# The second products of the last but one group in Strassen's form: a change at the end of a fused block kernel

## The chip, the cores and the metric

The kernel runs on one core of a Trainium2 chip. The metric is the device time of one execution in microseconds (us); smaller is better. Each time below is either that device time or a time in the trace of one profiled execution, counted from the start of its span.

The engines that matter here are TensorE (PE in the profile; its weight loads are PEld), VectorE (DVE), ScalarE (ACT), GpSimd (POOL) and SyncE (SP). PE writes its products into banks of its accumulator memory. There are eight, and each holds a tile of 128 x 512 numbers. DVE and ACT read them from there into the large on-chip memory. DMAs move data between that memory and DRAM, and one kind, issued from POOL, adds what it carries to what lies at its destination.

## The reference

The block is an FNet layer followed by a gated feed-forward layer, both with adaptive layer norms, for 2048 rows of 512 features and 1792 hidden features:

```python
x = A_x
mod = (_silu(c) @ w_mod).reshape(c.shape[0], 6, 1, -1)
sa, ca, ga, sb, cb, gb = (mod[:, 0], mod[:, 1], ..., mod[:, 5])
h = _layernorm(x) * (1 + ca) + sa
x = x + ga * _A_ref(h, ...)          # two DFTs as matrix products
h = _layernorm(x) * (1 + cb) + sb
gate = h @ w1
up = h @ w3
x = x + gb * ((_silu(gate) * up) @ w2)
```

The change lies wholly in the last line: `(silu(h @ w1) * (h @ w3)) @ w2`, scaled by `gb` and added to `x`.

## The kernel before

**Tiles.** Everything is held with features on the 128 partitions and rows along the free dimension. The 2048 rows are four tiles `t` of 512 rows. They go in two pairs, `PAIRS = ((0, 2), (1, 3))`. The 1792 hidden features are seven groups `g` of 256 (`NG` is 7), and the 512 output features are four columns `d` of 128 (`ND` is 4). Every product is made from three matmuls (`PASSES`): each operand is split into a high part, rounded by a copy on ACT, and a low part, the difference, taken on DVE.

**First products and second products.** An item `(g, pair)` is one group of hidden features for one pair of row tiles. Its first products are `h @ w1` and `h @ w3` for two row tiles and two blocks of 128 hidden features: eight block products in the plain form, seven in Strassen's form (in Winograd's order), with sums of operands formed ahead and sums of results formed behind. Most items make both in the seven-product form. These are the units `a1` to `a7` (w1) and `b1` to `b7` (w3) in the code, each of six matmuls. `result` takes what they give: it applies Silu to the gate, multiplies the two, and splits the product into high and low, as the operand of the second product.

**The second products** multiply that by `w2`. There are two forms:
- `down_unit`, the plain form: eight units for an item, one for each row tile `t` and output column `d`, each of six matmuls into one bank. Which bank is chosen by a counter, `turn[1]`, that only this function advances, modulo the length of the list `down_banks`. That list is `[6, 7]` during most of the phase and `[6, 7, 0, 1, 2]` from the last `a` unit of the last item on. The counter has advanced eight times for each item in this form.
- `seven_unit`, Strassen's form: seven units, in the order `ORDER7 = (2, 5, 3, 1, 6, 7, 4)`, each of six matmuls, three into bank 6 and then three into bank 7. Units 2, 5 and 1 begin a new sum in the two banks, and the units after each of them add to it. After every unit ACT copies both banks, scaled by `gb`, into a tile `y`, and POOL issues a DMA that adds `y` to its destination. `seven_parts` forms the seven right operands from the four results of the item, and `seven_jobs` prepares w2 for it: five jobs, against two in the plain form (`plain_jobs`).

`SEVEN` lists the items whose second products have Strassen's form: pair 1 and groups 0 to 4. The last two items, `(5, 1)` and `(6, 1)`, go by `down_unit`, in a form of their own (`own`): the running sum of `x` for row tiles 1 and 3, which till then lies in DRAM (`sums`), has been loaded into four tiles `xr` by `load_sums`, and DVE adds each bank to `xr` with one instruction. In the last item each such sum is followed at once by the DMA that writes it to the output.

**The order of the work** is written out by hand. For each item the strings `head` and `body` in the loop at the end of `folded` list the units: `a6` is unit 6 of w1 of this item, `-b7` is unit 7 of w3 of the item before, and `y` is the next unit of the queue `seconds`. That queue is filled after an item's unit `b3`: with seven entries for an item in `SEVEN`, otherwise with eight. Every engine then runs its instructions in the order in which the code issued them, and waits at the first that isn't ready.

Within a unit the order is this: `delayed()` first issues what earlier units put off (`behind(k, f)` has `f` run at the start of the k-th unit after this), then the six matmuls, then the reading of the bank, and last `beside`, which issues a few preparing jobs from the queue `jobs` if their estimated costs fit a budget of the unit. So the split of the `b3` results into high parts, put off by one unit, stands on ACT ahead of the copies of the next unit.

The preparation of w3 for the next item (`weight_jobs(i + 1, "w3")`: a high part, four short sums, a low part, the high and the low part of the sums) is put in the queue after `b6`.

`judge` compares sums of squares, collected earlier, that decide whether the fast form of the kernel was allowed; it is a chain of short DVE instructions and one memset on POOL. It runs at the unit at which nine second products of the last item's queue are left.

Of the kernel before, what the change touches and what calls it, by code (L numbers as in the profile page):

```python
# [12 lines left out]
OP = mybir.AluOpType  # L13
# [8 lines left out]
NT = S // N  # L22
ND = D // P
NG = F // (2 * P)
# [18 lines left out]
def folded(nc, pools, c, cp, wmr, wmc, x, xt, ctr, cti, wdr, wdi, w1, w3, w2, out):  # L43
# [39 lines left out]
    def cols(i):  # L83
        return slice(i * P, (i + 1) * P)
# [27 lines left out]
    done = set()  # L112
# [683 lines left out]
    xr = {}  # L796
# [17 lines left out]
    PAIRS = ((0, 2), (1, 3))  # L814
    h2h, h2l = {}, {}
    xc, sums = {}, {}
# [308 lines left out]
    def down_unit(g, pair, t, d, key):  # L1125
        last = g == NG - 1

        own = pair == 1 and g >= NG - 2
        if not own and d % 2 == 0:
            ys[0] = take(F32, "y")  # L1130

        parts = 2 if own and last and (t, d) == (NT - 1, ND - 1) else 1
        for n in range(parts):
            at = slice(n * N // parts, (n + 1) * N // parts)
            to = bank(down_banks[turn[1] % len(down_banks)])[:, at]
            turn[1] += 1
            for q in range(2):
                product(
                    to,
                    [u[:, q, cols(d)] for u in wuse[key]],  # L1140
                    [hf[g, t, q][:, b, at] for b in range(2)],
                    q == 0,
                    q == 1,
                )
            if own:
                xs = xr[t][d // 2][:, d % 2, at]
                nc.vector.scalar_tensor_tensor(
                    xs, to, gb[:, d : d + 1], xs, op0=OP.mult, op1=OP.add
                )
                if last:  # L1150
                    nc.sync.dma_start(out[t, d, :, at], xs)
            else:
                if pair == 0 and 1 <= g * ND + d <= 4:
                    nc.vector.tensor_scalar(
                        ys[0][:, d % 2, :], to, gb[:, d : d + 1], None, op0=OP.mult
                    )
                else:
                    copy_by(ys[0][:, d % 2, :], to, gb[:, d : d + 1])
        if not own and d % 2 == 1:
            y = ys.pop(0)  # L1160
            nc.gpsimd.dma_start(sums[t, d // 2], y, accum_op=OP.add)  # L1161
            behind(4, lambda: give(y))
            if last:
                behind(8, lambda i=d // 2: store(t, i))
        if d == ND - 1:
            for q in range(2):
                give(hf.pop((g, t, q)))
            if t == PAIRS[pair][1]:
                give_w(key)
            if pair == 1 and g == NG - 3:  # L1170
                load_sums(t)
# [51 lines left out]
    TO = {1: 0, 6: 0, 7: 0, 4: 0, 2: 1, 5: 2, 3: 2}  # L1223
    state, vs = {}, {}

    SEVEN = [(g, 1) for g in range(NG - 2)]
    ORDER7 = (2, 5, 3, 1, 6, 7, 4)
    LEFT7 = {1: "h0", 2: "h2", 4: "h3", 5: "s0", 6: "s1", 7: "s2", 3: "s3"}
    TO7 = {2: (0, 0), 5: (1, 1), 3: (0, 1), 1: (0, 0), 6: (0, 1), 7: (1, 1), 4: (1, 0)}
# [101 lines left out]
    def seven_unit(g, pair, n, key):  # L1331
        new = n in (1, 2, 5)
        if new:
            banks7[:] = [bank(6), bank(7)]
        y = take(F32, "y")
        which, k = TO7[n]
        t = PAIRS[pair][k]
        names = ("h", "l") if LEFT7[n][0] == "h" else ("sh", "sl")
        u = right7.pop(((g, pair), n))
        for e, to in enumerate(banks7):  # L1340
            at = int(LEFT7[n][1]) * HALF + e * P
            product(
                to,
                [flat(wuse[key][x])[:, at : at + P] for x in names],
                [u[:, b, :] for b in range(2)],
                new,
                True,
                not new,
            )
            d = 2 * which + e  # L1350
            copy_by(y[:, e, :], to, gb[:, d : d + 1])
        give(u)
        nc.gpsimd.dma_start(sums[t, which], y, accum_op=OP.add)  # L1353
        behind(4, lambda: give(y))
        if n == ORDER7[-1]:
            for x in wuse.pop(key).values():
                give(x)
            if g == NG - 3:
                for t in PAIRS[pair]:
                    load_sums(t)  # L1360
# [330 lines left out]
    def beside(us, used):  # L1691
        advance(us - used[0], us - used[1], jobs)
        if not jobs:
            advance(0.0, 0.0)
# [9 lines left out]
    def down(g, pair, *which):  # L1704
        key = which[-1]
        drain(lambda: (key, "l") in done, jobs)
        delayed()
        if (g, pair) in SEVEN:
            seven_unit(g, pair, *which)
        else:  # L1710
            down_unit(g, pair, *which)
        beside(1.36, USED["own" if pair == 1 and g >= NG - 2 else "y"])

    for w in ("w1", "w3"):
        load_w((w, 1))
# [33 lines left out]
    def early_w3(i):  # L1749
        return items[i][1] == 1  # L1750

    def unit(kind, i, n):
        g, pair = items[i]
        more = i + 1 < len(items)
        if n == 1:
            drain(lambda: ("ready", i, "w1" if kind == "a" else "w3") in done, jobs)
        if (kind, i, n) == ("a", 0, 6):
            drain(lambda: ("t", 0, 4) in done)
        if (kind, i, n) == ("a", turning, 1):
            drain(lambda: not background)  # L1760
        if kind == "a" and i == turning and n in (4, 5, 6, 7):
            drain(lambda: ("t", 1, {6: 2, 5: 1, 7: 3, 4: 4}[n]) in done, jobs)
        delayed()
        factor(i, "w1" if kind == "a" else "w3", n)
        if (kind, n) == ("a", 1):
            load_w(("w1", *items[i + 1]) if more else ("w2", g, pair))
        if (kind, n) == ("a", 6):
            load_w(("w2", g, pair))
        if not more and kind == "a" and state[i, "w1"]["n"] == 7:
            down_banks[:] = [6, 7, 0, 1, 2]  # L1770
        if (kind, n) == ("a", 7 if i == turning else 3) and more:
            load_w(("w3", *items[i + 1]))
            weight_jobs(i + 1, "w1")
        if (kind, n) == ("b", 2):
            (seven_jobs if (g, pair) in SEVEN else plain_jobs)(("w2", g, pair))
        if (kind, n) == ("b", 3):
            if i + 2 == turning:
                drain(lambda: ("xc", 3) in done)
                for at in ((1, 0), (1, 1), (3, 1)):
                    chunk_parts(background, *at, 3)  # L1780
                sums_of.append(pair_sums(background, 1))
            if i + 1 == turning:
                other_operands()
            if more and not early_w3(i):
                weight_jobs(i + 1, "w3")
            if (g, pair) in SEVEN:
                seconds.extend((g, pair, n, ("w2", g, pair)) for n in ORDER7)
            else:
                for t in PAIRS[pair]:
                    seconds.extend((g, pair, t, d, ("w2", g, pair)) for d in range(ND))  # L1790
        if (kind, n) == ("b", 6) and more and early_w3(i):
            weight_jobs(i + 1, "w3")
        beside(1.36, FACTOR[kind][n])

# [3 lines left out]
    for i in range(len(items)):  # L1798
        body = "a6 a5 y y a7 y a3 y a4 y b1 y b2 y b6 b5 y"
        if i and items[i - 1] in SEVEN:  # L1800
            body = "a6 a5 a7 y a3 a4 y b1 b2 y b6 b5 y"
        if i == turning + 1:
            body = "a6 a5 y a7 a3 y a4 b1 y b2 b6 y b5"
        spread = i > 1 and items[i - 2] in SEVEN
        if spread and i < len(items) - 1:
            body = body.replace("a6", "a6 y", 1)
        if i == len(items) - 2:
            body = "a6 y a5 y a7 a3 y a4 b1 y b2 b6 y b5"
        if i == turning:
            body = "y y y y y a6 y a5 y a7 y b1 b2 a4 b6 a3 b5"  # L1810
        if i == len(items) - 1:
            body = "a6 a5 b1 a7 a3 b2 a4 y b6 y b5 y b7 y b4 y y b3 y y y y y y y y y y"
        head = "-b7 a1 -b4 -b3 a2 " if i == turning else "-b7 a1 a2 -b4 -b3 " if i else "a1 a2 "
        if spread and i < len(items) - 1:
            head = "-b7 a1 y a2 -b4 y -b3 "
        if i == len(items) - 1:
            head = "-b7 y a1 a2 y -b4 y -b3 "
        for at in (head + body).split():
            if at == "y":
                if (i, len(seconds)) == (len(items) - 1, 9):  # L1820
                    judge()
                if (i, len(seconds)) == (len(items) - 1, 4):
                    tc.mark_branch_hint_location("general", hint="LikelyTaken")
                down(*seconds.popleft())
            elif at[0] == "-":
                unit(at[1], i - 1, int(at[2]))
            else:
                unit(at[0], i, int(at[1]))
# [804 lines left out]
```

## Time and profile before

| what | value |
|---|---|
| device time, median of 3 runs | 691.38 us |
| lowest and highest of the 3 | 690.79 and 692.02 us |
| device time of the profiled execution | 690.63 us |
| span of its trace | 688.8 us |
| PE busy | 672.4 us, 98% of the span |
| DVE busy | 586.8 us, 85% |
| ACT busy | 451.2 us, 65% |
| POOL busy | 132.2 us, 19% |
| mean rate of the DMAs | 170 GB/s |

The device time holds about 1.8 us more than the span, which runs from the first to the last event of the trace. PE is busy nearly all the time. Its busy time is only a rough measure, because matmuls overlap: a matmul of 512 columns is shown with some 390 ns, but the next one starts some 227 ns after it. How well PE is used is therefore read from the starts of the matmuls, in the view that lists instructions in order of time.

A line of that view gives the start in us, the duration in us, the engine, the line of the code, the operation, the tile written and the tiles read, the shapes, the count, and in brackets the idle time of the engine before it with what ended it.

### The profile page before, as it was taken

Reading aid. Unit: us, or ns where it says so; the run is one execution under the profiler, and the core shown is the slowest. Engines: PE = TensorE matmul, PEld = TensorE weight load, DVE = VectorE, ACT = ScalarE, POOL = GpSimd, SP = SyncE. Lnnn points to the kernel's source line nnn. Section 1 sums busy time; section 2 is a strip of 40 time slices with the busy share of each in tenths; the row PEclk is TensorE's granted clock in tenths of the full one; section 3 lists DMA queues with packets and bytes.
Section 4 is the critical chain, followed back from the end, with each engine's and each line's share of the span. In section 5 each row is a group of like instructions: output and inputs, shape, how many; then the busy total and the mean of one; then the engine's idle time right before and its main releaser. Section 6 shows DMA issues by size and latency. Waiting matters only on the chain.

```text
span 688.8 us, 9035 instructions
## 1 busy us (share of the span) xinstructions
PE 672.4 (98%) x3122; PEld 557.4 (81%) x3122; DVE 586.8 (85%) x945; ACT 451.2 (65%) x751; POOL 132.2 (19%) x156
## 2 busy tenths in 40 slices
PE   6999999999999999999999999999999999999996
PEld 4898788888888888888788888887887888888785
DVE  5999769998999987989997989787998979888465
ACT  4998956455343665663577767867687887877620
POOL 1320162543435000100101001011011112221100
PEclk9999999999999999999999999999999999999998
DMA  8740299787679440274767666475859998999713
GB/s 264 224 124 1 54 368 339 249 297 258 197 287 291 154 151 30 46 139 122 119 141 141 150 153 121 94 128 118 267 108 183 175 203 167 181 214 173 179 45 127
DMA packets 40837, 116.80 MB, mean 170 GB/s; under 512 B 5200, under 2 KB 5456, under 8 KB 40784
## 3 DMA queue, kind: packets, MB, share of 16 engines
q0 software_dynamic: 14512, 50.86, 36.9%
q1 hardware_dynamic: 25840, 63.98, 28.1%
q10 hardware_dynamic: 432, 1.31, 0.6%
q8 instruction: 26, 0.43, 0.3%
q14 instruction: 27, 0.22, 0.1%
HBM read 76.81 MB, written 41.42 MB: 172 GB/s over the span
## 4 chain that ended last, share of the span: by engine, by line
PE 84%; DVE 9%; ACT 4%; issue 1%; DMA 1%; SPq 0%; DVEq 0%; ACTq 0%
PE bank L100 54%; PE bank L750 26%; PE bank L559 2%; PE bank L598 1%; ACT hm L501 1%; DMA x<-in_x 1%; DVE xr L806 1%; DVE st L449 1%; PE bank L576 1%; DVE v L96 1%; DVE hl L90 0%; DVE ul L90 0%; DVE x L93 0%; ACT hh L87 0%; DVE w3s L90 0%
## 5 line engine op out<-in xcount | busy, mean ns | idle before, releaser
L100 PE MATMUL bank<-hf,w2h 128*128 128x512 f32 (+1 forms) x352 | 108.3, 389 | 0.0
L87 ACT ACTIVATE hf<-v 128x512 fp32r<-128x512 f32 x71 | 44.4, 631 | 66.7 <-DVE v L96 53.9
L335 ACT ACTIVATE y<-bank,gb 128x512 f32<-128x512 f32 x118 | 76.5, 682 | 3.9 <-PE bank L100 3.6
L100 PEld LDWEIGHTS bank<-hf,w2h 128*128 128x128 f32 x352 | 65.6, 188 | 15.4 <-ACT y L335 1.5
L1161 POOL DMA_DIRECT2D sum<-y x28 | 24.0, 857 | 240.7 <-ACT y L335 124.5
L100 PE MATMUL bank<-hf,w2l 128*128 128x512 f32 (+1 forms) x176 | 68.1, 387 | 0.0
L90 DVE TENSOR_TENSOR hf<-v,hf 128x512 fp32r<-128x512 f32 x71 | 48.7, 685 | 10.6 <-ACT hf L87 10.5
L1353 POOL DMA_DIRECT2D sum<-y x35 | 29.8, 852 | 128.3 <-ACT y L335 120.8
L87 ACT ACTIVATE x<-bank 128x512 f32<-128x512 f32 x72 | 41.7, 591 | 13.6 <-PE bank L100 12.7
L750 PE MATMUL bank<-d,uh 128*128 128x512 f32 x128 | 49.9, 390 | 0.0
L750 PE MATMUL bank<-l,us 128*128 128x512 f32 x128 | 49.9, 390 | 0.0
L750 PE MATMUL bank<-d,us 128*128 128x512 f32 x128 | 49.9, 390 | 0.0
L750 PE MATMUL bank<-bh,us 128*128 128x512 f32 x128 | 49.9, 390 | 0.0
L750 PE MATMUL bank<-bh,ul 128*128 128x512 f32 x128 | 49.8, 389 | 0.0
L750 PE MATMUL bank<-l,uh 128*128 128x512 f32 x128 | 49.8, 389 | 0.0
L170 POOL DMA_INDIRECT re<-in_ctr,mirror x32 | 35.7, 1115 | 66.6 <-ACT im L188 40.1
L170 POOL DMA_INDIRECT im<-in_cti,mirror x32 | 32.9, 1028 | 33.4 <-DVE l L90 8.9
L100 PEld LDWEIGHTS bank<-hf,w2l 128*128 128x128 f32 x176 | 33.1, 188 | 6.6
L93 DVE TENSOR_TENSOR v<-bank,x 128x512 f32<-128x512 f32 x36 | 24.7, 686 | 15.6 <-PE bank L100 14.0
L1245 ACT ACTIVATE v<-v 128x512 f32<-128x512 f32 x36 | 22.6, 629 | 22.7 <-DVE v L93 22.4
L93 DVE TENSOR_TENSOR x<-bank,x 128x512 f32<-128x512 f32 x36 | 24.7, 685 | 14.5 <-PE bank L100 13.7
L188 ACT ACTIVATE im<-l 128x512 f32<-128x512 f32 x16 | 10.1, 632 | 32.4 <-DVE d L93 15.5
(260 smaller groups left out, 1922.4 us busy)
## 6 DMA issues: line engine op xcount, KB each, us to landing
sum<-y POOLq DMA_DIRECT2D x63, 512.0 KB, 5.7
w<-in_w SPq DMA_DIRECT2D x42, 512.0 KB, 4.8
re<-in_ctr SPq DMA_DIRECT2D x32, 256.0 KB, 5.8
im<-in_cti SPq DMA_DIRECT2D x32, 256.0 KB, 5.3
wmc<-in_wmc SPq DMA_DIRECT2D x8, 512.0 KB, 7.2
sum<-xr SPq DMA_DIRECT2D x8, 512.0 KB, 5.6
x<-in_x SPq DMA_DIRECT2D x11, 256.0 KB, 4.5
xr<-in_xt SPq DMA_DIRECT2D x8, 256.0 KB, 7.1
```

Of the source, the lines that this page charges most:

```text
L87: nc.scalar.activation(dst, src, AF.Copy, scale=scale)
L90: nc.vector.tensor_tensor(out=dst, in0=a, in1=b, op=OP.subtract)
L93: nc.vector.tensor_tensor(out=dst, in0=a, in1=b, op=OP.add)
L100: nc.tensor.matmul(acc, lhs[a], rhs[b], start=first and n == 0, stop=last and n == len(PASSES) - 1, skip_group_check=more,)
L170: nc.gpsimd.indirect_dma_start(dst, None, rows, bass.IndirectOffsetOnAxis(ap=at, axis=0))
L188: nc.scalar.activation(to, src.bitcast(F32), AF.Square, accum_out=chk[:, kind, KINDS.index(m), n : n + 1],)
L335: nc.scalar.activation(dst, src, AF.Identity, scale=by)
L559: nc.tensor.matmul(halves(hb[k])[:, m, :], sides((hh, hl)[a][k])[:, dt, m, :], wu[dt][:, b, m, :], start=False, stop=dt % 2 == 1 and n == ...
L750: nc.tensor.matmul(acc[what, e], lhs, rhs, start=begin and i == 0, stop=(end or (turn and what == "x")) and i == len(terms) - 1, skip_grou ...
L1161: nc.gpsimd.dma_start(sums[t, d // 2], y, accum_op=OP.add)
L1245: behind(k != 0 or q == 0, lambda: nc.scalar.activation(v, src, AF.Silu))
L1353: nc.gpsimd.dma_start(sums[t, which], y, accum_op=OP.add)
```

## The change

There are four edits.

1. `SEVEN` takes in group 5, so the item `(5, 1)` makes its second products by seven units. Only the last item still has the form `own`. For group 5 the adding DMA goes to the tiles `xr` on the chip instead of `sums` in DRAM.
2. In the last item the second products of row tile 1 are parted: first columns 0 and 1 of tile 1, then all four of tile 3, and then columns 2 and 3 of tile 1. The halved last unit moves with it (`final`).
3. The last item's `body` is written anew: `a7` comes ahead of `b1`, the first `y` one unit earlier (ahead of `a4`), there is one `y` between `b4` and `b3` in place of two, and nine behind `b3` in place of ten. `judge` runs at the third unit of group 5's second products.
4. For the last item, w3's preparation is queued after the previous item's `b7` in place of its `b6`.

```diff
-        own = pair == 1 and g >= NG - 2
+        own = pair == 1 and g == NG - 1
...
-        parts = 2 if own and last and (t, d) == (NT - 1, ND - 1) else 1
+        final = (t, d) == ((PAIRS[1][0] if own else PAIRS[pair][1]), ND - 1)
+        parts = 2 if own and final else 1
...
-            if t == PAIRS[pair][1]:
+            if final:
                 give_w(key)
...
-    SEVEN = [(g, 1) for g in range(NG - 2)]
+    SEVEN = [(g, 1) for g in range(NG - 1)]
...
-        nc.gpsimd.dma_start(sums[t, which], y, accum_op=OP.add)
+        to = xr[t][which] if g == NG - 2 else sums[t, which]
+        nc.gpsimd.dma_start(to, y, accum_op=OP.add)
...
-        beside(1.36, USED["own" if pair == 1 and g >= NG - 2 else "y"])
+        beside(1.36, USED["own" if pair == 1 and g == NG - 1 else "y"])
...
-                for t in PAIRS[pair]:
-                    seconds.extend((g, pair, t, d, ("w2", g, pair)) for d in range(ND))
-        if (kind, n) == ("b", 6) and more and early_w3(i):
+                t0, t1 = PAIRS[pair]
+                places = [(t, d) for t in (t0, t1) for d in range(ND)]
+                if not more:
+                    places = places[:2] + places[4:] + places[2:4]
+                seconds.extend((g, pair, t, d, ("w2", g, pair)) for t, d in places)
+        if (kind, n) == ("b", 7 if i + 2 == len(items) else 6) and more and early_w3(i):
             weight_jobs(i + 1, "w3")
...
-            body = "a6 a5 b1 a7 a3 b2 a4 y b6 y b5 y b7 y b4 y y b3 y y y y y y y y y y"
+            body = "a6 a5 a7 b1 a3 b2 y a4 y b6 y b5 y b7 y b4 y b3 y y y y y y y y y"
...
-                if (i, len(seconds)) == (len(items) - 1, 9):
+                if (i, len(seconds)) == (len(items) - 1, 5) and "judged" not in done:
+                    done.add("judged")
                     judge()
```

## The prediction

> **What bounds the kernel now.** I read the page's busy times first, then the chain that ended last, then two stages of the end in order of time.
>
> ```profile
> span 688.8 us, 9035 instructions
> PE 672.4 (98%) x3122; PEld 557.4 (81%) x3122; DVE 586.8 (85%) x945; ACT 451.2 (65%) x751; POOL 132.2 (19%) x156
> PE 84%; DVE 9%; ACT 4%; issue 1%; DMA 1%; SPq 0%; DVEq 0%; ACTq 0%
> ```
>
> PE sets the time. So a matmul taken out is worth its full place, but only where PE isn't made to wait for something new. The chain of work, asked for the last 69 us, shows where it waits already:
>
> ```profile
> 629.12 0.03 DVE v L96
> ...
> 629.73 1.22 DVE w2l L90
> 630.95 0.34 DVE w3s L93
> ...
> 634.08 1.21 DVE w3sl L90
> 635.28 0.61 DVE x L93
> ...
> 635.92 0.70 DVE v L96
> ...
> 636.64 0.03 ACT hf L87
> 636.67 0.51 issue
> 637.18 0.68 ACT y L335
> 637.86 0.04 issue
> 637.90 3.01 PE bank L100 x12
> ...
> 640.93 41.18 PE bank L100 x186
> ```
>
> Here the pattern that decides my forecast is seen whole. DVE is late (preparing w2 and w3). So the product `v` of `-b7` is late, ACT's split into `hf`, first in ACT's queue, is late, the copies of the bank into `y` behind it are late, and PE, which needs that bank for the next `y` unit, starts 0.04 us after the copy. A second such stall ends at 640.93. The matmuls around both, in order of time:
>
> ```profile
> 637.42 0.39 PE L100 MATMUL bank<-h2h,w1l 128*128 128x512 f32 x1
> 637.90 0.74 PE L100 MATMUL bank<-hf,w2sh 128*128 128x512 f32 x2
> ...
> 639.40 0.39 PE L100 MATMUL bank<-th,w3h 128*128 128x512 f32 x1
> ...
> 666.90 0.39 PE L100 MATMUL bank<-h2h,w3sh 128*128 128x512 f32 x1
> ...
> 668.26 0.62 PE L100 MATMUL bank<-hf,w2h 128*128 128x512 f32 x2
> ```
>
> The rows at 666.90 and 668.26 begin two successive units: a unit of six matmuls takes 1.36 us. The unit at 637.90 should have begun at 637.42 + 0.23 = 637.65 and took 1.50 us, so a stall costs its wait and some 0.14 us more. Between 640.93 and the end there is no gap.
>
> **Part by part.** *Removed:* eight units become seven, so 1.36 us of PE goes. Eight additions on DVE go too, which is not the bound there.
>
> *Added beside PE.* ACT gets 14 copies into `y`, three splits more and one preparing copy; DVE gets four differences, three low parts, four short sums and a low part of 1024 columns. The stage has room:
>
> ```profile
> 650.00:660.00 10.00, 10.00 (x46) 8.29 (x45) 5.76 (x8) 4.53 (x7) 0.00 (x0) 1.00 0.45 160
> 660.00:670.00 10.00, 10.00 (x46) 8.29 (x45) 7.68 (x12) 1.35 (x3) 0.00 (x0) 1.00 0.00 0
> ```
>
> The fifth figure, ACT, is 4.53 and 1.35 us of each 10. In sum nothing overflows. What counts is the order at four places.
>
> *Place 1, w2's and w3's preparation, at 629.73.* After the sum and product of `b2` DVE now has all of w2's Strassen preparation, and w3's moved behind `-b7`. The item before has the same operations for (4,1), without a gap on DVE:
>
> ```profile
> 599.23 0.69 DVE L96 TENSOR_TENSOR v<-v,x 128x512 f32<-128x512 f32 x1
> 599.84 0.42 DVE L93 TENSOR_TENSOR w2s<-w 128x256 f32<-128x256 f32 x1
> ...
> 601.30 1.22 DVE L90 TENSOR_TENSOR w2l<-w,w2h 128x1024 fp32r<-128x1024 f32 x1
> 602.44 0.68 DVE L90 TENSOR_TENSOR hf<-v,hf 128x512 fp32r<-128x512 f32 x1
> 603.04 1.22 DVE L90 TENSOR_TENSOR w2sl<-w2s,w2sh 128x1024 fp32r<-128x1024 f32 x1
> 604.18 0.41 DVE L93 TENSOR_TENSOR w3s<-w 128x256 f32<-128x256 f32 x1
> ...
> 606.78 0.68 DVE L93 TENSOR_TENSOR x<-bank,x 128x512 f32<-128x512 f32 x1
> 607.50 0.69 DVE L96 TENSOR_TENSOR v<-v,x 128x512 f32<-128x512 f32 x1
> ```
>
> From start to start: four short sums 1.46 us (599.84 to 601.30), a low part of 1024 columns 1.14, one of 512 columns 0.60, a sum with its product 0.72 + 0.61. The new order from 629.73: w2's short sums 1.46, low part 1.14, `hf` of `b2` 0.60, low part of the sums 1.14, sum and product of `-b7` 1.33, w3's short sums 1.46, low part 1.14, `hf` of `-b7` 0.60, low part of the sums 1.14. Together 10.01, so to 639.74. (The budgets of the units let w3's last job out at `a1`, ahead of the sum of `a2`.) The product of `-b7` is now ready at 635.49 instead of 636.62, and the copies behind it no longer hold up the unit at 637.64: that stall goes. What is late next is the sum of `a2`. Before, it starts at 638.95:
>
> ```profile
> 638.95 0.69 DVE L93 TENSOR_TENSOR v<-bank,x 128x512 f32<-128x512 f32 x1 [0.95 <-ACT x L87]
> 639.67 0.63 ACT L1245 ACTIVATE v<-v 128x512 f32<-128x512 f32 x1 [0.76 <-DVE v L93]
> 640.21 1.25 ACT L335 ACTIVATE y<-bank,gb 128x512 f32<-128x512 f32 x2
> ```
>
> The Silu follows 0.72 later, the copies 0.54 after that, and PE at 640.93. With the sum at 639.74 that chain is 0.79 later, and PE starts at 641.72. **+0.79 us**, with the old stalls already counted in the 640.93. With w3 still behind `b6` it would have been `-b7` that came late; the move trades one stall for another.
>
> *Place 2, new `y` units after `b2` and `b7`.* Take the sum, product and split behind `b3`:
>
> ```profile
> 668.46 0.69 DVE L93 TENSOR_TENSOR x<-bank,x 128x512 f32<-128x512 f32 x1 [0.61 <-PE bank L100]
> 669.19 0.69 DVE L96 TENSOR_TENSOR v<-v,x 128x512 f32<-128x512 f32 x1
> ...
> 669.91 0.63 ACT L87 ACTIVATE hf<-v 128x512 fp32r<-128x512 f32 x1 [4.11 <-DVE v L96]
> ```
>
> The split begins 1.65 us after the unit's last matmul made way (668.26). With copies behind it, the first begins at 1.65 + 0.54 = 2.19 and ends at 2.87 (0.68 each), the second ends 1.25 after 2.19, at 3.44. Before, no ACT copies stood here, because the plain units of (5,1) were read by DVE. In `b2 y a4 y` and `b7 y b4 y` the next `y` is due 2.72 us after, and gets bank 6 at 2.91: 0.19 and the 0.14 of a restart, twice. **+0.66 us.**
>
> *Place 3, the first plain unit of the last item.* The counter that chooses banks no longer advances for (5,1). At the last item's first unit it has stood at 56 (seven items of pair 0 with eight units each), not 64. 56 modulo 5 is 1, and the second of `[6, 7, 0, 1, 2]` is bank 7; before it was bank 2. Bank 7 has just been filled by the last Strassen unit, one unit after `b3`. Its copy is the second one behind the split: it ends 3.44 us after `b3`, and PE may start at 3.48. It was due at 1.36. So 2.12 us of wait and 0.14: **+2.26 us.** All other units wait behind it, PE being in order.
>
> *Place 4, costs taken as nothing.* `judge`'s DVE chain moves to a stretch before `b7`, where DVE is idle (7.68 of 10 us includes the additions now gone); were that cover gone, its 3 us would delay `b7`'s split. The seven additions into `xr` no trace shows: a DMA that adds into the on-chip memory. The nearest rows:
>
> ```profile
> L1353 POOL DMA_DIRECT2D sum<-y x35: 847/855/860, 505.0 to 643.8; - x35
> DMA to landing us min/median/max: 2.6/5.4/10.3
> ```
>
> Issued some 5.2 us after `b3` (3.44, a hand-over and 0.86 on POOL), the last lands 8 to 16 after it, 10.6 at the median. DVE needs it for column 2 of tile 1, the seventh plain unit: 3.48 + 7 x 1.36 = 13 after `b3`. I take it as hidden; the upper end costs 3 us, the lower gains nothing because nobody waits for it. The other six have longer.
>
> *Sum:* 0.79 + 0.66 + 2.26 - 1.36 = **+2.35 us**. The profiled execution took 690.63 us, so 693.0 on its account; it is the low end of the runs, and on the median of 691.38 the forecast is **693.7 us**.
>
> **The rivals.**
>
> *A. The bank wait doesn't bite, and the kernel is faster.* If the split of `b3` did not stand ahead of the copies, bank 7's copy would follow its matmuls (1.36 + about 0.2 + 0.68), a wait under 0.9 us; with a bank other than 7 there is none. Then 1.36 is earned, and the two old stalls may go as well (waits of 0.25 and, at 640.93 against 639.40 + 1.36, of 0.17, with 0.14 each: 0.70): 691.38 - 1.36 - 0.70 = 689.3, up to 690.3 with a short wait. It decides if place 3's wait is below 1 us. Against it: the chain at 636.64 to 637.90 shows just this order in ACT's queue. 13%.
>
> *B. Place 1 costs nothing.* If w3's last low part is issued behind `a2`'s sum, that sum starts at 639.74 - 1.14 = 638.60, and the unit that I have at 641.72 starts at 640.58, 0.35 before the old 640.93: 691.38 - 0.35 + 0.66 + 2.26 - 1.36 = 692.6; 691.9 with place 2 empty too. No change that can be told. 23%.
>
> *C. The additions into `xr` come late*, by up to 3 us: 693.7 to 696.7. It decides from a landing above 7.8 us. 5%.
>
> *D. PE's clock drops in the new gap.* At the very end PE stops at 682.1:
>
> ```profile
> 684.00:685.00 1.00, 0.00 (x0) 0.00 (x0) 0.00 (x0) 0.00 (x0) 0.00 (x0) 1.00 0.26 80
> 685.00:686.00 1.00, 0.00 (x0) 0.00 (x0) 0.00 (x0) 0.00 (x0) 0.00 (x0) 0.62 0.00 0
> ```
>
> The granted clock is full for 3 us of idling and falls after that. [...] 2%. [...]
>
> **How the numbers follow.** My forecast has 57%, B 23%, A 13%, C and D together 7%. About 0.2%, 1.4 us, is what a measurement of this kernel can tell from no change. Faster is A: 0.13. Within is B and a little of the forecast's lower edge: 0.25. Slower is the rest: 0.62. The range reaches from below B, with no stall left in the head and place 2 empty (691.38 - 0.70 + 2.26 - 1.36 = 691.6, less 0.6, by which the lowest of the three runs lies under their median, so 691.0) to the forecast with a somewhat late addition (694.8), and leaves out A and most of C and D.
>
> **What would show it.** In the changed profile: a gap of about 2.1 us on PE just ahead of the first `hf,w2h` unit of the last item, ended by ACT's copy into `y`; a gap of about 1.4 us in the head, at the last second product of group 4, where before there were two of 0.25 and 0.17; gaps of about 0.2 us at the second and the last but one unit of group 5; DVE's last additions never ended by a DMA. If the first gap is missing or short, place 3 is wrong and A holds. If the gap in the head is missing, B holds.

## The result and the profile after

The changed kernel is slower: 695.74 us in the median of 8 runs (693.65 to 697.05), the kernel before 691.70 us in the median of 8 runs of the same comparison (690.79 to 694.69). The ratio on record is 1.0051, with a 95% interval of 1.0035 to 1.0067 (it isn't the quotient of the two medians, which is 1.0058). Forecast were 693.7 us and a range of 691.0 to 694.8. The direction was right, and the measured time lies above the range. In a second comparison the same kernel took 694.49 us (12 runs) against 691.88, ratio 1.0032 (1.0020 to 1.0044).

The page of the changed kernel's profiled execution, which was one of the longest of the 8 (697.04 us), its parts 1 and 4:

```profile
span 695.3 us, 9062 instructions
PE 674.5 (97%) x3116; PEld 557.0 (80%) x3116; DVE 588.6 (85%) x949; ACT 462.6 (67%) x769; POOL 138.8 (20%) x163
PE 75%; DVE 12%; ACT 5%; DMA 4%; issue 2%; SPq 1%; ACTq 0%; DVEq 0%
```

There are six matmuls fewer, as planned, and ACT has 11.4 us more. The chain that ended last leaves PE more often: 75% of the span against 84%. Here is that chain from 640 us on (start, duration, what), cut to the steps around PE's stretches:

```profile
642.41 1.22 DVE w3sl L90
643.63 0.61 DVE v L93
...
644.26 0.63 ACT v L1246
644.89 0.59 ACT y L335
645.48 0.04 issue
645.52 11.23 PE bank L100 x48
...
658.35 0.63 ACT hf L87
658.98 0.58 ACT y L335
659.57 0.04 issue
659.61 8.51 PE bank L100 x36
...
669.66 0.63 ACT hf L87
670.30 0.58 ACT y L335
670.88 0.04 issue
670.92 3.05 PE bank L100 x12
...
675.45 0.63 ACT hf L87
...
676.55 0.69 ACT y L335
677.24 0.04 issue
677.28 11.26 PE bank L100 x54
```

Each of PE's stretches begins 0.04 us after a copy into `y`, and that copy stood behind a Silu or a split that had waited for DVE. These are the three places of the forecast. In order of time, PE shows the last of them like this:

```profile
674.93 0.39 PE L100 MATMUL bank<-hf,w2l 128*128 128x512 f32 x1
677.28 0.74 PE L100 MATMUL bank<-hf,w2h 128*128 128x512 f32 x2 [1.97 <-ACT y L335]
```

From 674.93 the next matmul was due 0.23 later; it came 2.13 us after that. Read in the same way, the four gaps are 1.38 us (forecast 1.36), 0.31 and 0.26 (0.19 each) and 2.13 (2.12). After each, the first two matmuls take 0.11 us longer (0.74 against 0.62 or 0.63), a slow restart.

How much longer is the last stage itself? Take it from an instruction that both kernels run unchanged, the first matmul of `a7` of the item (5, 1), to the end of the last addition on DVE. First the two instructions before, then after:

```profile
618.60 0.39 PE L100 MATMUL bank<-th,w1sh 128*128 128x512 f32 x1
...
682.13 0.48 DVE L1147 SCALAR_TENSOR_TENSOR xr<-bank,gb,xr 128x256 f32<-128x256 f32 x1 [0.23 <-PE bank L100]
```

```profile
622.38 0.39 PE L100 MATMUL bank<-th,w1sh 128*128 128x512 f32 x1
...
688.57 0.48 DVE L1148 SCALAR_TENSOR_TENSOR xr<-bank,gb,xr 128x256 f32<-128x256 f32 x1 [0.23 <-PE bank L100]
```

Before, the stage ended at 682.13 + 0.48 and took 64.01 us; now it takes 689.05 - 622.38 = 66.67. So the changed stage costs **2.66 us**. The other 3.78 us of the two spans' difference (622.38 against 618.60) arose before any changed instruction.

### The profile page after: what moved, and what is told of

Read it like the earlier page. It is cut to its first block, busy times and chain, and to the rows that moved or that the text cites. A ratio compares the mean times of both kernels' runs of the same rounds, so it can differ in the third digit from the quotient of the medians.

```text
span 695.3 us, 9062 instructions
## 1 busy us (share of the span) xinstructions
PE 674.5 (97%) x3116; PEld 557.0 (80%) x3116; DVE 588.6 (85%) x949; ACT 462.6 (67%) x769; POOL 138.8 (20%) x163
## 4 chain that ended last, share of the span: by engine, by line
PE 75%; DVE 12%; ACT 5%; DMA 4%; issue 2%; SPq 1%; ACTq 0%; DVEq 0%
PE bank L100 52%; PE bank L750 19%; PE bank L559 2%; DMA scr<-in_c 2%; DMA wmr<-in_wmr 1%; PE bank L598 1%; DVE v L96 1%; DVE x L93 1%; ACT y L335 1%; ACT hm L501 1%; DVE xr L806 1%; DMA re<-in_ctr 1%; DVE d L93 1%; DVE ul L90 1%; DVE l L90 1%
## 5 line engine op out<-in xcount | busy, mean ns | idle before, releaser
L100 PE MATMUL bank<-hf,w2h 128*128 128x512 f32 (+1 forms) x332 | 102.3, 389 | 3.2 <-ACT y L335 3.2
L335 ACT ACTIVATE y<-bank,gb 128x512 f32<-128x512 f32 x132 | 85.7, 682 | 4.1 <-PE bank L100 3.6
L87 ACT ACTIVATE hf<-v 128x512 fp32r<-128x512 f32 x74 | 46.1, 631 | 58.2 <-DVE v L96 46.8
L100 PEld LDWEIGHTS bank<-hf,w2h 128*128 128x128 f32 x332 | 61.8, 188 | 18.0 <-ACT y L335 5.0
L100 PE MATMUL bank<-hf,w2l 128*128 128x512 f32 (+1 forms) x166 | 64.2, 387 | 0.0
L90 DVE TENSOR_TENSOR hf<-v,hf 128x512 fp32r<-128x512 f32 x74 | 50.6, 686 | 11.9 <-ACT hf L87 11.8
L100 PEld LDWEIGHTS bank<-hf,w2l 128*128 128x128 f32 x166 | 31.2, 188 | 6.3
```

Of the source, the lines that this page charges most:

```text
L87: nc.scalar.activation(dst, src, AF.Copy, scale=scale)
L90: nc.vector.tensor_tensor(out=dst, in0=a, in1=b, op=OP.subtract)
L100: nc.tensor.matmul(acc, lhs[a], rhs[b], start=first and n == 0, stop=last and n == len(PASSES) - 1, skip_group_check=more,)
L335: nc.scalar.activation(dst, src, AF.Identity, scale=by)
```

## The experiments

The theory is that of the forecast: the unit saved is worth 1.36 us, and three places where PE waits for ACT's copies cost more than that. A rival that the result leaves is that something else makes the rest: the start of the kernel, the clock behind the long gap, the additions into `xr`. The stage is measured as above; each kernel stands against the kernel before on the same chip.

| kernel | median us, runs | ratio to before (95% interval) | stage us |
|---|---|---|---|
| before | | | 64.01 |
| changed | 695.74, 8 | 1.0051 (1.0035 to 1.0067) | 66.67 |
| e1_bank | 691.98, 12 | 1.0009 (0.9998 to 1.0020) | 64.37 |
| e2_w3 | 693.72, 10 | 1.0030 (1.0012 to 1.0048) | 66.65, with 1.5 at half clock |
| e3_split_b3 | 693.10, 12 | 1.0020 (1.0003 to 1.0038) | 65.60 |
| e4_all | 689.87, 12 | 0.9977 (0.9963 to 0.9990) | 61.95 |
| f1_same | 694.49, 12 | 1.0032 (1.0020 to 1.0044) | 68.22, with 1.55 at half clock |
| f2_fill | 694.44, 12 | 1.0036 (1.0023 to 1.0049) | 66.63 |
| f3_longer | 696.85, 6 | 1.0059 (1.0040 to 1.0077) | 69.22, with 1.6 at half clock |
| f4_w3_b6 | 695.89, 6 | 1.0056 (1.0034 to 1.0078) | 67.71 |
| g1_plain_w3 | 692.89, 12 | 1.0018 (1.0004 to 1.0033) | 65.21 |
| g2_all_again | 689.42, 7 | 0.9963 (0.9948 to 0.9977) | 61.95 |
| h1_plain_mended | 691.82, 12 | 0.9990 (0.9975 to 1.0006) | 63.31 |

**Another bank for the first plain unit.**

```diff
-            down_banks[:] = [6, 7, 0, 1, 2]
+            down_banks[:] = [7, 0, 1, 2, 6]
```

> The changed kernel with the banks of the last item's plain units listed as 7, 0, 1, 2, 6, so that the first of them takes bank 0. If the wait for bank 7 is what stands ahead of that unit (2.13 us in the changed kernel's profile, and 0.11 of a slow restart), the gap is gone, the last matmul comes 2.2 us earlier counted from the end of b2, and the time falls by about 2.2 us. If the gap has another cause (the splits or the additions of group 5 being late), a gap of 1 to 2 us stays and the time falls by less than 1 us.

On PE the first plain unit now follows at once:

```profile
671.55 0.39 PE L100 MATMUL bank<-hf,w2l 128*128 128x512 f32 x1
671.77 0.39 PE L100 MATMUL bank<-hf,w2h 128*128 128x512 f32 x1
```

The gap is gone, the three others stay, and the stage is 2.30 us shorter than the changed kernel's. So the bank wait alone is worth nearly all that the changed stage costs over the stage before. In time the kernel comes from 1.0051 or 1.0032 down to 1.0009.

**w3's preparation later.**

```diff
-        if (kind, n) == ("b", 7 if i + 2 == len(items) else 6) and more and early_w3(i):
+        if (kind, n) == ("b", 6) and i + 2 < len(items) and early_w3(i):
             weight_jobs(i + 1, "w3")
+        if (kind, n) == ("a", 2) and not more:
+            weight_jobs(i, "w3")
```

> The changed kernel with w3's preparation for the last item queued after its a2 in place of the previous item's b7. If DVE's preparation ahead of a2's sum makes the gap of 1.38 us in the head, that gap goes and nothing takes its place: 1.4 to 1.5 us less time. If DVE's work is only moved on, a gap of like size shows at a later unit y or at b1, and the time stays within 0.5 us of the changed kernel's.

The gap of 1.38 us is gone and none takes its place. But the stage is as long as before the edit, because something else happened behind the gap of 2.13 us. The matmuls in order of time, and a stretch behind the gap (the figure before the last two is the granted clock):

```profile
672.52 0.87 PE L100 MATMUL bank<-hf,w2h 128*128 128x512 f32 x2 [1.97 <-ACT y L335]
673.19 0.63 PE L100 MATMUL bank<-hf,w2l 128*128 128x512 f32 x1
673.62 1.05 PE L100 MATMUL bank<-hf,w2h 128*128 128x512 f32 x2
...
676.97 0.62 PE L100 MATMUL bank<-hf,w2h 128*128 128x512 f32 x2
```

```profile
673.00:676.30 3.30, 3.30 (x10) 2.52 (x9) 0.75 (x1) 0.00 (x0) 0.62 (x1) 0.50 0.98 185
```

From 673.19 to 673.62 a matmul takes 0.43 us, nearly twice its 0.227, and the clock is at half for some 3.4 us. That is rival D of the forecast, the clock that drops for the new gap, though the gap is only 2.1 us long. Without the 1.5 us that this costs the stage would be about 65.1, 1.5 less than the changed kernel's, as expected. The time alone doesn't show it: 1.0030, against 1.0051 and 1.0032 for the changed kernel.

**The split behind the copies.** In the last item the split of `b3`'s product waits one unit more:

```diff
-        behind(1, highs)
-        behind(2, lows)
+        put_off = i == len(items) - 1 and (q, k) in ((0, 1),)
+        behind(1 + put_off, highs)
+        behind(2 + put_off, lows)
```

> The changed kernel with the split of b3's product in the last item put off by one unit more, so that the two copies of the last Strassen unit stand ahead of it on ACT; the bank stays 7. If the split at the head of ACT's queue makes most of the wait, the gap of 2.13 us falls to about 0.9 (the unit's own matmuls, 0.2 us, and a copy of 0.68) and the time falls by about 1.2 us. If the bank alone decides, whatever stands ahead of its copies, the gap stays above 1.8 us.

The bank is still 7. ACT in order of time, and PE:

```profile
672.61 1.37 ACT L335 ACTIVATE y<-bank,gb 128x512 f32<-128x512 f32 x2 [1.23 <-PE bank L100]
673.87 0.62 ACT L87 ACTIVATE hf<-v 128x512 fp32r<-128x512 f32 x1
```

```profile
674.02 0.74 PE L100 MATMUL bank<-hf,w2h 128*128 128x512 f32 x2 [0.78 <-ACT y L335]
```

The copies now go ahead of the split, and the gap falls from 2.13 to 0.94 us, as expected. So both halves of place 3 are shown: the bank makes PE wait, and the split at the head of ACT's queue makes more than half of the wait.

**All three places mended:** the bank list of e1, the preparation of e2, and the splits of `b2` and `b7` put off as in e3, with `((0, 0), (1, 1))`.

> All three places mended: banks 7, 0, 1, 2, 6; w3 prepared after a2; the splits of b2 and b7 put off by one unit more. If the places are the whole loss of the last stage, no gap above 0.1 us is left on PE after 600 us, the work from b2 to the end is 4.5 us shorter than in the changed kernel and 2.0 us shorter than in the kernel before (1.36 for the unit saved and 0.70 for the old gaps), and the time is some 0.3% below the kernel before. If the change also slows the start of the kernel (the first 30 us, where the profiled run of the changed kernel had fallen 3.8 us behind before any changed instruction ran), the time comes out 0.5 to 2 us above that.

The chain of this kernel, from 615 us on, is one stretch of PE:

```profile
614.86 67.86 PE bank L100 x305
682.72 0.02 issue
682.74 0.48 DVE xr L1148
```

No gap is left. The stage takes 61.95 us, 4.72 less than the changed one and 2.06 less than the one before, and the kernel is faster than the kernel before in two comparisons: 0.9977 and, as g2_all_again, 0.9963. It is the fastest version found here.

**The changed kernel again.**

> The changed kernel once more, beside the next three. The gaps on PE should come back at the same places with the same lengths (1.38, 0.31, 0.26 and 2.13 us), since they come from the order of the instructions. If the gap of 2.13 us sometimes costs TensorE's clock, its runs spread towards longer times by up to 1.7 us more, and the time stands 3.0 to 3.5 us above the kernel before; if it never does, 2.5 us above.

The gaps come back to the hundredth: 1.38, 0.31, 0.26, 2.13. In this profile the clock did fall behind the last one:

```profile
676.50:679.90 3.40, 3.40 (x10) 2.66 (x9) 0.98 (x2) 0.00 (x0) 0.00 (x0) 0.50 1.01 193
```

The stage takes 68.22 us, 1.55 more than in the first profile of the same kernel, where the clock stayed up. By the medians the time is 2.6 us above the kernel before, near the 2.5 expected where the clock is never lost. The mean granted clock, which is on record for every run, says the same: in seven of the twelve runs it is 0.998 or 0.999. The profiles that show one stretch of 3.4 us at half speed before their last matmul (the changed kernel, e2_w3, e4_all, f3_longer) have 0.994 to 0.996 there, so by this estimate at most five of the twelve lost one, behind this gap or elsewhere.

**The gap filled with matmuls that nobody reads.**

```diff
+        if own and (t, d) == (PAIRS[1][0], 0):
+            spare = bank(0)
+            for _ in range(9):
+                nc.tensor.matmul(spare, wuse[key][0][:, 0, cols(0)], hf[g, t, 0][:, 0, :], ...)
```

> The changed kernel with nine matmuls into a spare bank, which nobody reads, put into the gap of 2.13 us: they take 9 x 0.227 = 2.0 us, so PE is busy there and everything behind starts when it did. If the gap costs only its own length, the time is that of the changed kernel (within 0.3 us). If the idling also lowers the clock in a part of the runs (the stretch of about 3.4 us at half speed that the profile of e2_w3 shows behind its gap, some 1.6 us long in cost), the time falls by 0.5 to 0.9 us, and no profile of this kernel shows a lowered clock behind the gap.

```profile
673.13 2.20 PE L1136 MATMUL bank<-hf,w2h 128*128 128x512 f32 x9
```

PE is busy through the gap and the clock stays up (behind it one matmul starts 0.23 us after another), but the time didn't fall: 1.0036 against 1.0032 for f1_same. The expectation of 0.5 to 0.9 us was missed. The mean granted clock agrees: it is 0.9964 over these twelve runs and 0.9971 over those of f1_same, so f1_same had not lost more of it than this kernel.

**A longer gap.** One copy of 1024 columns more on ACT, between the split and the copies:

```diff
+        if (g, n) == (NG - 2, 4):
+            more = take(F32R, "more")
+            copy(flat(more), flat(wuse[key]["h"]).bitcast(F32))
+            give(more)
```

> The changed kernel with one copy of 1024 columns more on ACT between the split of b3 and the two copies: the gap grows from 2.13 to about 3.1 us. [...] If the clock has nothing to do with the loss, the time rises by 0.95 us.

```profile
676.30 0.73 PE L100 MATMUL bank<-hf,w2h 128*128 128x512 f32 x2 [2.91 <-ACT y L335]
```

The gap is 3.07 us, and the clock fell in this profile: the stage is 69.22 us, 2.55 more than the changed kernel's first. In time the distance to f1_same is 0.0027, some 1.9 us; the intervals (1.0020 to 1.0044, 1.0040 to 1.0077) just touch. That agrees with 0.95 us for the gap and a clock lost more often, as does the mean granted clock, 0.9953 over the six runs against 0.9971 in f1_same, but six runs don't prove the second part.

**w3's preparation back behind `b6`.**

```diff
-        if (kind, n) == ("b", 7 if i + 2 == len(items) else 6) and more and early_w3(i):
+        if (kind, n) == ("b", 6) and more and early_w3(i):
```

> The changed kernel with w3's last preparation put back behind b6. Worked out in DVE's order, w3's short sums then stand ahead of the product of b7, but its low parts stay where they are, and a2's sum still starts after the same work: the gap of 1.38 us becomes two of about 0.6 each, ahead of the last but one and the last Strassen unit of group 4, and the time stays within 0.3 us of the changed kernel's. If the move was worth something by itself, the time rises by 0.5 us or more.

Missed: at place 1 stand gaps of 0.59 and 1.75 us instead of two of 0.6, the other places are as in the changed kernel, and the stage is 1.04 us longer than there. DVE shows what was overlooked, and below it ACT:

```profile
641.69 1.23 DVE L90 TENSOR_TENSOR w3sl<-w3s,w3sh 128x1024 fp32r<-128x1024 f32 x1 [1.06 <-ACT w3sh L87]
```

```profile
638.92 0.64 ACT L87 ACTIVATE hf<-v 128x512 fp32r<-128x512 f32 x1 [1.96 <-DVE v L96]
639.46 1.25 ACT L335 ACTIVATE y<-bank,gb 128x512 f32<-128x512 f32 x2
640.60 1.06 ACT L87 ACTIVATE w3sh<-w3s 128x1024 fp32r<-128x1024 f32 x1
```

The low part of w3's sums waits for their high part on ACT (`w3sh`). That stands behind two copies into `y` and the split of `-b7`'s product, which had waited for DVE. The lateness goes round, from DVE to ACT and back. So the move of w3 to `b7` is worth about 1 us by itself, where the forecast had seen a mere trade of stalls.

**The plain form with w3's preparation moved.** To have Strassen's form alone, the edit of e2 was made in the kernel before.

> The kernel before, with the second products of group 5 still in the plain form, and with w3's preparation for the last item queued after its a2. The two old gaps (0.26 and 0.18 us, with 0.11 of restart each) should go, and nothing take their place: 0.66 us less than the kernel before. If they were only moved, the time is that of the kernel before.

Missed. The old gaps went, but a new one of 1.76 us came:

```profile
645.91 1.23 DVE L90 TENSOR_TENSOR w3sl<-w3s,w3sh 128x1024 fp32r<-128x1024 f32 x1 [2.76 <-DMA sum<-y]
```

With the jobs in another order, w3's last part was given a tile of which a DMA was still reading a `y`; DVE waited for it, and all behind it in its queue.

> The changed kernel with all three places mended (e4_all), beside the one above. Both have no gap left on PE, so what parts them is the unit saved by Strassen's form: 1.36 us, and about 2.0 us under the kernel before. If Strassen's form costs something that the gaps don't show (the seven additions into xr, a later end), the two lie closer together than 1 us.

Because of that gap g1 doesn't answer this. In the next kernel w3's last part takes another tile:

```diff
         def sum_lows():
+            if (i, w) == (len(items) - 1, "w3"):
+                free.rotate(-1)
             use["sl"] = take(F32R, w + "sl")
```

> The kernel of g1_plain_w3, with w3's last part put into a tile whose last reader isn't a DMA under way. If the gap of 1.76 us there came from that tile alone, no gap is left on PE after 600 us and the time is 0.6 to 0.7 us below the kernel before; then the distance to the mended changed kernel (e4_all, g2_all_again) is the unit that Strassen's form saves, 1.36 us. If DVE is late for another reason, a gap above 1 us stays at the same unit and the time stays above the kernel before.

The chain from 615 us on is one stretch of PE again:

```profile
614.95 69.44 PE bank L100 x312
684.40 0.02 issue
684.42 0.48 DVE xr L1147
```

The stage takes 63.31 us: 0.70 less than before, as expected. In time no difference can be told (the interval is 0.9975 to 1.0006). The mended changed kernel's stage takes 61.95. The distance, 1.36 us, is exactly the unit that Strassen's form saves.

## Why the forecast was wrong

**What held.** The saving is 1.36 us (h1 against e4). Place 1 gave 1.38 us against 1.36, place 3 gave 2.13 against 2.12. e2 takes place 1 away by itself and e1 place 3. e4 takes away all, with place 2, which no run mended alone. Place 2 was undersized, 0.31 and 0.26 for 0.19 twice. Behind `b2` and `b7` the sum began 0.27 us after the unit's last matmul made way (656.85 after 656.58, 668.21 after 667.94), where the forecast's rows have 0.20, and the split of `b2` began 0.09 us after `v` was there, not 0.03. The additions into `xr` were hidden, as taken: nothing on DVE waits for one. They were even issued sooner than taken: the forecast's 5.2 us after `b3` leaves 0.9 for the hand-over to POOL, and the last one began 0.28 us after its copy (677.52 after 677.24). Only POOL waits for an addition, once:

```profile
L1355 POOL DMA_DIRECT2D xr<-y x7: 854/859/867, 660.4 to 677.5; - x7
...
POOL xr L1355: 1.7, 1
```

The sum of the steps was +2.35 us; the stage shows +2.66. Of the difference 0.19 is place 2 and 0.03 the two others. Most of the rest is the restarts: the changed stage takes 4.72 us more than that of e4, which has no gap, and the four gaps make 4.08 of it, so a restart cost 0.16 us, where the forecast had 0.14. The mechanism was right, then, and nearly the size.

**What failed** is the step from that sum to the runs: the upper end of the range, 694.8. It left room for a late addition alone, and put the spread of the runs at nothing there and rival D, the clock, at 2%.

First, the spread. The forecast took it from three runs, as 0.6 us below their median, and used it at the lower end only. In the later comparisons, with 17 to 33 runs of the kernel before each, its runs went from 690.42 to 694.82 us. The thirteen profiles show where: `a7` of the item (5, 1) starts between 618.60 (the kernel before, from which the sum was made) and 622.38 us (the changed kernel), though all instructions up to there are the same. Much of it is the first 15 us. The first transposes on PE, before and after:

```profile
8.92 0.72 PE L485 MATMUL bank<-ident,x 128*128 128x128 f32 x4 [1.81 <-DVE x L470]
```

```profile
10.48 0.72 PE L485 MATMUL bank<-ident,x 128*128 128x128 f32 x4 [2.40 <-DVE x L470]
```

In the second the first rows of `x` were ready 1.6 us later, and the granted clock then stood at half for 3.4 us:

```profile
11.40:14.80 3.40, 3.31 (x10) 1.74 (x9) 3.29 (x5) 2.30 (x5) 0.00 (x0) 0.50 1.05 245
```

Before, the same stretch has a clock of 1.00. e4_all was slowed in a like way: its first eight transposes take 1.95 us (10.43 to 12.38), those of the kernel before 1.03 (8.92 to 9.95). A late start falls on the plain form too: h1_plain_mended begins the first group of four copies into `hm` at 25.62 us, the kernel before at 24.13 and the changed one at 26.20. Why one execution starts later than another stays open. Nothing speaks for a start slowed by the change itself: in e1, e3, f2 and g1, in whose stage no clock was lost, the median differs from the kernel before by what the stage says, within 0.2 us (0.53 for 0.36, 1.65 for 1.59, 2.56 for 2.62, 1.06 for 1.20), though f4, g2 and e4 are 0.3 to 0.5 off and h1 is 1.1 off.

The median of the first 8 runs was 1.25 us above that of the next 12 runs of the same kernel, and the mean granted clock on record shows what went with it. By calculation one stretch of 3.4 us at half speed takes 0.0025 off it (half of 3.4, of 695). It is 0.9949 over the first 8 runs and 0.9971 over the next 12; the 0.0022 between them are about 1.5 us of lost clock in the mean of a run. The runs without a profile don't tell whether that was at the start or behind the gap; in the one of the eight that was profiled it was at the start. The second comparison's +2.2 us (ratio 1.0032) contains the forecast's +2.35 in its interval (+1.4 to +3.0), while the first one's (+2.4 to +4.6) begins just above it.

Second, the 2% for D was too low. Of the four profiles with the gap of 2.13 us, two (e2_w3, f1_same) fell to half clock behind it and two (the changed kernel, f4_w3_b6) did not; it costs 1.5 to 1.55 us where it happens. The rows of the kernel's end, from which the forecast read D, show a clock of 1.00 for some 3 us after PE's last matmul and a lower one after that; they don't show what a gap of 2.13 us does with matmuls behind it. That such a gap keeps the clock was the author's estimate. Even odds would add about 0.8 us to a mean; with them the expected time would have been near 694.5, within the range still, but with the starts' spread on top the range's upper end was too low. The runs put the odds lower, by an estimate from their mean clocks: of the 36 runs of kernels with this gap 22 have 0.996 or less, of the 171 runs of kernels without a gap above 1.8 us 65 have. If the two causes are independent, the gap lowers the clock in some 37% of the runs, with a wide margin at so few of them, which is worth about 0.6 us in the mean. How much of the first comparison's median is the gap's clock and how much the start's was not separated: f2_fill, which keeps the clock up behind the gap, was no quicker than f1_same.

**The rivals.** A and C did not happen. D did in some runs, at a cost of 1.5 to 1.55 us. B, a clean place 1, came about only in e2 and e4, by moving the preparation further. The trade-off that the forecast named for w3's move was read too cheaply, as f4 shows.

## What to carry to other kernels

Saving a unit of the bounding engine pays only if its last reader hands the bank back in time (here 1.36 us was saved, and PE waited 2.13 us for bank 7): list, for each unit, which bank it takes, who empties that bank, and what stands ahead of that reader in its engine's queue (with the split behind the copies that wait fell to 0.94 us). A counter that only one form of a unit advances shifts the banks of all later units when a form is changed, so work it out anew. Judge a small change by the stretch of the profile from an unchanged instruction to the end as well as by the time. Take the spread of the runs from many runs, not three, and allow for it at both ends of a range.

## What the runs showed of the hardware

TensorE's granted clock fell to half (0.50) behind a gap of 2.13 us in two of the four profiles that have one (e2_w3, f1_same) and behind the one of 3.07 us (f3_longer). It stayed at 1.00 behind the 2.13 us of the changed kernel and of f4_w3_b6 and behind the 1.38 us of the changed kernel, and behind the 1.75 us of f4_w3_b6 the matmuls kept their full pace, one in 0.23 us. The half speed lasted 3.4 us each time, the start of the changed kernel included, and cost 1.5 to 1.6 us behind the gaps. Why gaps of equal length end differently isn't shown.

A DMA from POOL that adds 512 KB into on-chip tiles landed in 6.0 us in the median, those that add into DRAM in 5.6 us in the same profile (of the changed kernel; the two kinds ran at different times, so the destination is not shown to be the reason):

```profile
sum<-y POOLq DMA_DIRECT2D x63, 512.0 KB, 5.6
...
xr<-y POOLq DMA_DIRECT2D x7, 512.0 KB, 6.0
```
